# Expert weights: twenty of 104 low parts on GpSimd, 26 high parts on VectorE, and the first layer's last block as three 224-column products

## Chip, cores and metric

The kernel runs on one core of one Trainium2 chip. The metric is the device time of one execution in microseconds (us); a kernel's time is the median of its runs.

## What is computed

Three stages follow each other, in float32: attention with normalised queries and keys, a mixture of eight experts in which each expert takes at most 224 of 1792 tokens, and an MLP with the activation h * cos(h). The change lies in the second stage.

```python
def _moe_ref(x, w_gate, w1, w2):
    N, D = x.shape                      # 1792, 768
    E = w_gate.shape[1]                 # 8 experts, w1 768x1024, w2 1024x768
    cap = N // E                        # 224
    order = np.argsort(-(x @ w_gate).flatten())
    ...                                 # tokens go to experts in this order, 224 each
    for e in range(E):
        mask = assigned == e
        h = np.maximum(x[mask] @ w1[e], 0.0)
        out[mask] = h @ w2[e]
    return out
```

After it comes `h = x @ w_in; (h * cos(h)) @ w_out` for all 1792 tokens.

## The kernel before

**Two plans.** The kernel writes no engine's order by hand. Every operation becomes a `Step` with the engines that could run it (`ways`), its cost, and what it reads and writes. `Plan.run` then simulates all engines by these costs, picks at each moment a step by its due time, and emits the instructions in that order; on the chip each engine runs its own queue in that order and waits where data is missing. There is one plan for attention and one, called `second`, for the rest. A step with two ways goes to the engine that would finish it first. For that comparison the VectorE way is charged an extra `prefer` times its cost; `prefer` is the first number of `TUNE_B`, 1.75 before. `P.either` makes a step with a VectorE and a GpSimd way, but only while `P.shared` is true, and `moe` sets it to False (just above `fetch(0)`), so no low part has two ways before.

**Precision.** TensorE multiplies in fp32r, which keeps the high part of a float32. So each operand x is split into a high part (a copy in fp32r) and a low part (x minus the high part), and a product is hi*hi + hi*lo + lo*hi.

**An expert.** For experts 1 to 7, `expert(t, j)` first does eight blocks f of w1 (128 columns each, six pieces d of 128 rows) and then six blocks d of w2 (eight pieces f). I write expert 3's blocks as f0 to f7 and d0 to d5, and one piece as d0:6. Expert 0's first layer has no split. For every split block:

- `whole` issues a load from HBM into a ring of four stage tiles `ws` (SyncE queue, in order),
- `weights` (L1217) makes the high part, `wx<-ws`, on ScalarE or VectorE (two ways, also before), and the low part, `wx<-ws,wx`, on VectorE; `wx` is a ring of four tiles,
- TensorE does `two` per piece: the high part against 448 columns (the tokens' high and low parts side by side), then the low part against 224 columns,
- `halves` adds the two 224-column halves of the accumulator: a ScalarE copy of one half to `sm`, a VectorE addition,
- ScalarE writes the high part of the result and VectorE the low part: `gh<-sm` and `gh<-sm,gh` for w1 (with the relu), `x2h` and `x2l` for w2.

The pieces of w2's first block need all eight results of w1; the plan lets TensorE run pieces of d1 before d0:6 and d0:7, since f6 and f7 are the last to come.

**Beside it.** The router for the expert after next (`Router.slow`) runs at the same time on VectorE: it sends candidates to DRAM (`rows<-vm`), reads them back into all partitions with eight broadcast loads (`AB<-rows`, SyncE queue), and then takes eight steps of comparing (`oh<-AB`), counting and a small product. GpSimd issues the gathers of an expert's tokens (`xr<-x,idx`) and the scatters of results (`out_dram<-xo,idx`) and has nothing else to do in this part. Two experts are followed by an MLP over their 448 tokens, four times.

Of the kernel before, what the change touches and what calls it, by code (L numbers as in the profile page):

```python
# [12 lines left out]
F32 = mybir.dt.float32  # L13
# [4 lines left out]
ALU = mybir.AluOpType  # L18
# [32 lines left out]
class Plan:  # L51
# [99 lines left out]
    def ring(self, pool):  # L151

        def make(name, n, shape, dt=F32):
            tiles = [pool.tile(shape, dt, name=f"{name}{i}") for i in range(n)]
            at = [0]

            def take():
                at[0] += 1
                return tiles[(at[0] - 1) % n]
            return take  # L160
        return make
# [540 lines left out]
CP, NCOL, E, CAP = 112, 16, 8, 224  # L702
# [402 lines left out]
CP, E, CAP, DM, F1, F2 = 112, 8, 224, 768, 1024, 2048  # L1105
KD, K1, K2 = DM // 128, F1 // 128, F2 // 128
PT = 2 * CAP
C1 = 6.28125
C2 = 2.0 * math.pi - C1
TUNE_B = (1.75, 0.8, 2.6, 0.6, 7.0, 9e9)  # L1110
RUSH = (15.0, 4.0, 5.0)
QUICK = (0, 1)
WARM_B = 24
# [2 lines left out]
TURN = 5  # L1116
EARLIER = 140
MAGS = 4
GROUPS = [[0, 1], [2, 3], [4, 5], [6, 7]]


def moe(tc, P, R, ident, x_rows, w1, w2, w_in, w_out, out, narrow):

    nc = tc.nc
    with ExitStack() as ctx:
        cst = ctx.enter_context(tc.tile_pool(name="m_cst", bufs=1))
        pp = ctx.enter_context(tc.tile_pool(name="m_ps", bufs=1, space=PSUM))
        v, sc = P.vector, P.scalar
# [12 lines left out]
        xe = cst.tile([128, KD, PT], F32R, name="xe")  # L1141
        xf = cst.tile([128, KD, CAP], F32, name="xf")
        xo = cst.tile([CP, 4, DM], F32, name="xo")
        mags = ring("na", MAGS, [128, 4, 128], I32)
        x2h = cst.tile([128, KD, PT], F32R, name="x2h")
# [56 lines left out]
        def whole(src, c0, n, keys):  # L1202

            s = stage()[:, 0:n]

            def load():
                w = src()
                nc.sync.dma_start(s, w[:, c0:c0 + 128].rearrange("(k p) n -> p k n", p=128))

            P.add([("SP", 0.46, load)], keys, [s], dma=n * 0.182)  # L1210
            return s

        def weights(src, c0, n, keys):

            s, x = whole(src, c0, n, keys), parts()[:, 0:n]
            hi, lo = x[:, :, 0], x[:, :, 1]
            P.add([("ACT", 0.093 + n * 0.1067, lambda: nc.scalar.activation(hi, s, AF.Copy)),  # L1217
                   ("DVE", 0.07 + n * 0.0667, lambda: nc.vector.tensor_copy(hi, s))], [s], [hi])
            v.tensor_tensor(lo, s, hi.bitcast(F32), op=ALU.subtract)
            return hi, lo  # L1220

        def ready(src, k0, n, keys):
# [6 lines left out]
        def fresh(d, k0):  # L1229
            x = parts()  # L1230
            for k in range(k0, k0 + K1, 4):
                i = narrow.at["wo", d, k]
                if i >= EARLY:
                    raw = stage().rearrange("p k n -> p (k n)").bitcast(I32).rearrange("p (k n) -> p k n", k=4)
                    narrow.piece(P, i, raw, mags(), x[:, k - k0:k - k0 + 4])
            return x[:, :, 0], x[:, :, 1]

        def block(f):
            P.begin()
            f()  # L1240
            P.finish()
            chain.append(P.steps[-1])

        def three(p, hi, lo, xh, xl, first, last):
            P.tensor.matmul(p, hi, xh, start=first, stop=False)
            P.tensor.matmul(p, hi, xl, start=False, stop=False)
            P.tensor.matmul(p, lo, xh, start=False, stop=last)

        def two(p, hi, lo, x, first, last):
            P.tensor.matmul(p, hi, x, start=first, stop=False)  # L1250
            P.tensor.matmul(p[:, 0:CAP], lo, x[:, 0:CAP], start=False, stop=last)

        def halves(p):
            y = sums()
            sc.activation(y, p[:, CAP:PT], AF.Copy)
            v.tensor_tensor(y, p[:, 0:CAP], y, op=ALU.add)
            return y

        def expert(t, j):
            def of(w):  # L1260
                return lambda: w[bass.ds(ev[t], 1)].rearrange("o k n -> (o k) n")

            for f in range(K1):
                if t == 0:
                    s = whole(of(w1), f * 128, KD, [f"ev{t}"])
                    p = acc()[:, 0:CAP]
                    for d in range(KD):
                        block(lambda: P.tensor.matmul(p, s[:, d], xf[:, d], start=d == 0,
                                                      stop=d == KD - 1))
                else:  # L1270
                    hi, lo = weights(of(w1), f * 128, KD, [f"ev{t}"])
                    p = acc()[:, 0:PT]
                    for d in range(KD):
                        block(lambda: two(p, hi[:, d], lo[:, d], xe[:, d], d == 0, d == KD - 1))
                    p = halves(p)
                a, b = hT[:, f, 0:CAP], hT[:, f, CAP:PT]
                sc.activation(a, p, AF.Relu)
                v.scalar_tensor_tensor(b, p, 0.0, a.bitcast(F32), op0=ALU.max, op1=ALU.subtract)
            o = j * CAP
            for d in range(KD):  # L1280
                hi, lo = weights(of(w2), d * 128, K1, [f"ev{t}"])
                p = acc()[:, 0:PT]
                for f in range(K1):
                    block(lambda: two(p, hi[:, f], lo[:, f], hT[:, f], f == 0, f == K1 - 1))
                p = halves(p)
                a, b = x2h[:, d, o:o + CAP], x2l[:, d, o:o + CAP]
                sc.activation(a, p, AF.Copy)
                v.tensor_tensor(b, p, a.bitcast(F32), op=ALU.subtract)

        def mlp(grp, ahead):  # L1290
# [15 lines left out]
            for d in range(KD):  # L1306
                if grp is GROUPS[0] and narrow.at["wo", d, 0] >= EARLY:
                    both = [fresh(d, k0) for k0 in range(0, K2, K1)]
# [4 lines left out]
                if d == TURN:  # L1313
                    ahead()
                cut = w // 2 if last and grp is GROUPS[-1] else w
                for a in range(0, w, cut):
# [30 lines left out]
        def fetch(t, step=None):  # L1347
            if t < E:
                P.rush = RUSH[min(t, 2)]
                route(t, step)  # L1350
                P.rush = 0.0

        fetch(0)
        for grp in GROUPS:
            for j, t in enumerate(grp):
                if j:
                    fetch(t)
                expert(t, j)
            behind = chain[-EARLIER]
            mlp(grp, lambda: fetch(grp[-1] + 1, behind))  # L1360
        P.run(zip(chain, chain[1:]), *TUNE_B)

# [64 lines left out]
```

## Time and profile before

| | us |
|---|---|
| median of 3 runs | 1168.14 |
| lowest, highest | 1165.21, 1170.52 |
| the profiled execution | 1162.75 |
| its span, first to last instruction | 1160.8 |

The profile names groups of instructions as `out<-in` without buffer numbers. "Idle before" an instruction, in brackets, is how long its engine stood still and what ended that. PE is TensorE's matmuls, DVE is VectorE, ACT ScalarE, POOL GpSimd, SP SyncE's queue of DMA issues. A matmul's own duration includes its pipeline; how fast they follow each other is read from their starts.

### The profile page before, as it was taken

The numbers are of one execution on the slowest core, as the hardware profiler recorded it, in microseconds if no ns is written. First come the engines' busy times: TensorE is split into PE (matmuls) and PEld (weight loads), VectorE is DVE, ScalarE is ACT, GpSimd is POOL, SyncE is SP. The second block draws the span as 40 slices with busy tenths as digits, with TensorE's granted clock in tenths as the row PEclk, the third lists the DMA queues.
The fourth block names the chain that finished last, engine by engine and source line by source line (L and its number), as shares of the span: only waits on it lengthen the run. The fifth ranks groups of instructions, "written<-read, shape, count | busy, mean of one in ns | idle before, by whom it ended". The sixth has DMA issues, their size and how long they took to land.

```text
span 1160.8 us, 22190 instructions
## 1 busy us (share of the span) xinstructions
PE 1108.4 (95%) x7944; PEld 906.6 (78%) x7944; DVE 899.8 (78%) x2477; ACT 646.4 (56%) x1575; POOL 137.6 (12%) x288
## 2 busy tenths in 40 slices
PE   7999999999994989999999999999999999999996
PEld 5465665555552879899899899899899989999996
DVE  7888998999977978996997897578889578856401
ACT  4787787676663356663556574246666235746400
POOL 5361332331000000000001000001000000100001
PEclk9999999999996999999999999999999999999998
DMA  7236575655751589779669668838867956866761
GB/s 215 66 114 224 156 236 181 191 169 177 234 206 61 151 216 270 267 240 304 224 163 266 206 208 259 303 107 233 245 215 231 298 204 171 239 207 217 244 217 48
DMA packets 180815, 237.58 MB, mean 205 GB/s; under 512 B 14113, under 2 KB 156897, under 8 KB 175073
## 3 DMA queue, kind: packets, MB, share of 16 engines
q1 hardware_dynamic: 178144, 225.15, 62.6%
q0 software_dynamic: 2560, 11.01, 3.5%
q8 instruction: 62, 1.02, 0.4%
q14 instruction: 49, 0.39, 0.1%
HBM read 199.52 MB, written 36.52 MB: 203 GB/s over the span
## 4 chain that ended last, share of the span: by engine, by line
PE 45%; DVE 3%; DMA 2%; ACT 1%; issue 1%; POOL 0%; POOLq 0%; SPq 0%; ACTq 0%; DVEq 0%
PE acc L47 44%; DMA ws<-in_moe_w_dram 2%; PE tr L47 1%; DVE wx L47 1%; DVE na L47 1%; ACT wx L1217 1%; PE rt L47 1%; DVE oh L47 0%; DVE xo L47 0%; POOL out_dram L1337 0%; DVE xe L47 0%; POOLq L1423 0%; DVE gh L47 0%; DVE ind L47 0%; DVE sm L47 0%
## 5 line engine op out<-in xcount | busy, mean ns | idle before, releaser
L47 PE MATMUL acc<-gh,wx 128*128 128x448 f32 (+1 forms) x1568 | 360.4, 344 | 4.1 <-DVE gh L47 3.6
L47 PEld LDWEIGHTS acc<-gh,wx 128*128 128x128 f32 x1568 | 264.8, 190 | 22.1 <-DVE gh L47 5.8
L47 PE MATMUL acc<-x2h,wx 128*128 128x448 f32 x768 | 222.3, 368 | 0.0
L47 PEld LDWEIGHTS acc<-x2h,wx 128*128 128x128 f32 x768 | 144.5, 188 | 11.2
L47 PE MATMUL acc<-gl,wx 128*128 128x448 f32 (+1 forms) x400 | 143.2, 358 | 0.0
L47 PE MATMUL acc<-x2l,wx 128*128 128x448 f32 x384 | 140.1, 365 | 0.0
L47 DVE TENSOR_TENSOR wx<-ws,wx 128x768 fp32r<-128x768 f32 (+1 forms) x104 | 112.3, 1080 | 26.5 <-ACT wx L1217 23.7
L1217 ACT ACTIVATE wx<-ws 128x768 fp32r<-128x768 f32 (+1 forms) x104 | 97.8, 940 | 28.8 <-DMA ws<-in_moe_w_dram 13.3
L47 ACT ACTIVATE pf<-st 112x448 f32<-112x448 f32 x192 | 93.7, 539 | 34.1 <-PE st L47 33.4
L47 DVE TENSOR_REDUCE cm<-s 128x1 f32<-128x448 f32 x168 | 100.2, 618 | 14.1 <-PE s L47 12.1
L47 PE MATMUL acc<-xe,wx 128*128 128x448 f32 (+1 forms) x672 | 107.3, 320 | 0.1
L47 ACT ACTIVATE r<-r 128x448 f32<-128x448 f32 x128 | 74.1, 579 | 57.8 <-DVE r L47 56.0
L47 PEld LDWEIGHTS acc<-xe,wx 128*128 128x128 f32 x672 | 100.6, 189 | 5.3 <-DVE wx L47 0.6
L47 PE MATMUL st<-qq,kk 64*112 64x448 f32 x576 | 89.1, 387 | 0.9 <-ACT pf L47 0.9
L47 ACT ACTIVATE oh<-oh 128x896 bf16<-128x896 bf16 x48 | 45.6, 950 | 73.8 <-DVE oh L47 73.7
L1168 POOL DMA_INDIRECT xr<-x,idx x16 | 15.5, 966 | 582.7 <-issue 198.8
L47 PE MATMUL po<-pf,vr 112*64 112x448 f32 x384 | 83.4, 552 | 0.3 <-ACT pf L47 0.3
L47 PEld LDWEIGHTS acc<-gl,wx 128*128 128x128 f32 x400 | 75.4, 189 | 4.7
L47 PEld LDWEIGHTS acc<-x2l,wx 128*128 128x128 f32 x384 | 72.2, 188 | 5.2
L47 PEld LDWEIGHTS st<-qq,kk 64*112 64x112 f32 x576 | 49.1, 171 | 18.1 <-ACT pf L47 5.6
L47 ACT ACTIVATE sq<-qk 112x64 f32<-112x64 f32 (+1 forms) x195 | 57.6, 303 | 8.2 <-DVE rt L47 4.1
L47 DVE COPY xo<-tr 112x512 f32<-112x512 f32 (+1 forms) x25 | 16.5, 664 | 58.0 <-PE tr L47 56.4
(251 smaller groups left out, 1831.9 us busy)
## 6 DMA issues: line engine op xcount, KB each, us to landing
wx<-w_in SPq DMA_DIRECT2D x64, 768.0 KB
wx<-w_out SPq DMA_DIRECT2D x44, 1024.0 KB
ws<-in_moe_w_dram SPq DMA_DIRECT2D x64, 384.0 KB
ws<-in_moe_w_dram SPq DMA_DIRECT2D x48, 512.0 KB
nr<-in_moe_w_in_dram SPq DMA_DIRECT2D x32, 384.0 KB
w_in<-nr SPq DMA_DIRECT2D x32, 384.0 KB
nr<-in_moe_w_out_dram SPq DMA_DIRECT2D x16, 512.0 KB
w_out<-nr SPq DMA_DIRECT2D x16, 512.0 KB
```

The source lines that it names most:

```text
L47: self.plan.add([(self.eng, self.plan.cost(self.eng, name, out, r, kw), lambda: f(*args, **kw))], r, w)
L1168: P.add([("POOL", 2.1 - 0.9 * h, lambda x=x, h=h: nc.gpsimd.indirect_dma_start(out=x, out_offset=None, in_=x_rows, in_offset=bass.Indirect ...
L1217: P.add([("ACT", 0.093 + n * 0.1067, lambda: nc.scalar.activation(hi, s, AF.Copy)), ("DVE", 0.07 + n * 0.0667, lambda: nc.vector.tensor_co ...
```

## The change

One tuning number and two places in `moe` change:

```diff
-TUNE_B = (1.75, 0.8, 2.6, 0.6, 7.0, 9e9)
+TUNE_B = (0.8, 0.8, 2.6, 0.6, 7.0, 9e9)
...
+SHORT = (K1 - 1,)
...
-            v.tensor_tensor(lo, s, hi.bitcast(F32), op=ALU.subtract)
+            P.shared = True
+            P.either("tensor_tensor", lo, s, hi.bitcast(F32), op=ALU.subtract)
+            P.shared = False
...
-                    for d in range(KD):
-                        block(lambda: two(p, hi[:, d], lo[:, d], xe[:, d], d == 0, d == KD - 1))
-                    p = halves(p)
+                    if f in SHORT:
+                        p = p[:, 0:CAP]
+                        for d in range(KD):
+                            block(lambda: three(p, hi[:, d], lo[:, d], xe[:, d, 0:CAP], xe[:, d, CAP:PT], d == 0, d == KD - 1))
+                    else:
+                        for d in range(KD):
+                            block(lambda: two(p, hi[:, d], lo[:, d], xe[:, d], d == 0, d == KD - 1))
+                        p = halves(p)
```

The low parts get a second way, GpSimd. `prefer` also weighs the high parts' VectorE way, so these move too. In the built program 20 of the 104 low parts stand on GpSimd (13 of w1, 7 of w2) and 26 of the 104 high parts on VectorE (18 of w1, 8 of w2), where before all high parts stood on ScalarE and all low parts on VectorE. Block f7 of experts 1 to 7 accumulates in 224 columns and has no `halves`. Attention's order is the same, instruction by instruction; in the rest the plan sets all engines anew.

VectorE at the end of expert 3's first layer, before. `wx2`, `wx3`, `wx0`, `wx1` with x8x128 are the low parts of d0, d1, d2, d3; the `sm` rows are the additions for f5, f6, f7; the `gh` rows are the low parts of f4, f5, f6, f7; `oh` is the router's first comparison:

```order
L47 TENSOR_TENSOR wx2_4610<-ws2_4606,wx2_4610 128x8x128
L47 TENSOR_TENSOR sm1_4619<-acc3_4599,sm1_4619 128x224
L47 SCALAR_TENSOR_TENSOR gh_4631<-sm0_4618,gh_4631 128x224
L47 TENSOR_TENSOR wx3_4611<-ws3_4607,wx3_4611 128x8x128
L47 SCALAR_TENSOR_TENSOR gh_4631<-sm1_4619,gh_4631 128x224
L47 TENSOR_TENSOR sm0_4618<-acc0_4596,sm0_4618 128x224
L47 TENSOR_TENSOR wx0_4608<-ws0_4604,wx0_4608 128x8x128
L47 TENSOR_TENSOR sm1_4619<-acc1_4597,sm1_4619 128x224
L47 TENSOR_TENSOR wx1_4609<-ws1_4605,wx1_4609 128x8x128
L47 SCALAR_TENSOR_TENSOR gh_4631<-sm0_4618,gh_4631 128x224
L47 SCALAR_TENSOR_TENSOR gh_4631<-sm1_4619,gh_4631 128x224
L47 TENSOR_SCALAR oh_4651<-AB_4650,b0_80 128x896
```

The same place with the change (the `gh` rows are f5, f6, f7; `CAST` is the high part of d3):

```order
L47 TENSOR_TENSOR wx2_4610<-ws2_4606,wx2_4610 128x8x128
L47 TENSOR_TENSOR sm1_4619<-acc3_4599,sm1_4619 128x224
L47 TENSOR_TENSOR sm0_4618<-acc0_4596,sm0_4618 128x224
L47 SCALAR_TENSOR_TENSOR gh_4631<-sm1_4619,gh_4631 128x224
L47 TENSOR_SCALAR oh_4651<-AB_4650,b0_80 128x896
L47 TENSOR_TENSOR wx0_4608<-ws0_4604,wx0_4608 128x8x128
L1219 CAST wx1_4609<-ws1_4605 128x8x128
L47 SCALAR_TENSOR_TENSOR gh_4631<-sm0_4618,gh_4631 128x224
L47 SCALAR_TENSOR_TENSOR gh_4631<-acc1_4597,gh_4631 128x224
```

The low parts of d1 and d3 and the addition for f7 are gone from VectorE; the router's comparison and a high part have come in ahead of f6 and f7, and f7's low part reads the accumulator.

GpSimd's queue with the change, from the low part of expert 3's f4 to the gathers for expert 4 (before, nothing stood between the scatters and these gathers). The low parts are f4, f7, d1 and d3:

```order
L47 TENSOR_TENSOR wx2_4610<-ws2_4606,wx2_4610 128x6x128
L47 TENSOR_TENSOR wx1_4609<-ws1_4605,wx1_4609 128x6x128
L47 TENSOR_TENSOR wx3_4611<-ws3_4607,wx3_4611 128x8x128
L47 TENSOR_TENSOR wx1_4609<-ws1_4605,wx1_4609 128x8x128
L1169 DMA xr0_4620<-x_66,idx4_4637 112x768
L1169 DMA xr1_4621<-x_66,idx4_4637 112x768
```

Four low parts have come in behind the scatters of the first MLP; expert 5 has the same four.

SyncE's queue for expert 1, before (register moves and the load of f4 left out). The w1 rows are the loads of f1, f3, f5, f6, f7:

```order
L1208 DMA ws3_4607<-in_moe_w1_dram 128x6x128
...
L1208 DMA ws1_4605<-in_moe_w1_dram 128x6x128
...
L1208 DMA ws3_4607<-in_moe_w1_dram 128x6x128
L997 DMA rows_71<-vm_4652 112x8x16
...
L1208 DMA ws0_4604<-in_moe_w1_dram 128x6x128
L1000 DMA AB_4650<-rows_71 16x1792 x8
...
L1208 DMA ws1_4605<-in_moe_w1_dram 128x6x128
```

The same queue with the change; the w1 rows are the loads of f0, f2, f1, f3, f4:

```order
L1209 DMA ws2_4606<-in_moe_w1_dram 128x6x128
L997 DMA rows_71<-vm_4652 112x8x16
...
L1209 DMA ws0_4604<-in_moe_w1_dram 128x6x128
...
L1209 DMA ws3_4607<-in_moe_w1_dram 128x6x128
L1000 DMA AB_4650<-rows_71 16x1792 x8
...
L1209 DMA ws1_4605<-in_moe_w1_dram 128x6x128
...
L1209 DMA ws2_4606<-in_moe_w1_dram 128x6x128
```

The router's broadcasts have moved from between f6 and f7 to between f1 and f3. For experts 3 and 5 they stand where they stood, between f5 and f6.

## Rows read from the trace of the kernel before

**Rows 1.** The page, busy time, share of the span and instructions of two engines.
```profile
PE 1108.4 (95%) x7944; PEld 906.6 (78%) x7944; DVE 899.8 (78%) x2477; ACT 646.4 (56%) x1575; POOL 137.6 (12%) x288
```
**Rows 2.** Windows, second layers of experts 3, 5, 7: length; busy PE, PEld, DVE, ACT, POOL; clock.
```profile
636.25:653.57 17.32, 15.57 (x98) 14.28 (x97) 15.47 (x35) 11.17 (x24) 0.00 (x0) 1.00 0.67 207
825.39:842.59 17.20, 15.57 (x98) 14.28 (x97) 15.69 (x35) 11.04 (x24) 0.00 (x0) 1.00 0.69 216
1014.51:1029.60 15.09, 15.09 (x98) 14.26 (x97) 8.98 (x17) 7.19 (x16) 0.00 (x0) 1.00 0.60 189
```
**Rows 3.** Timeline of PE, the waits in the second layers of experts 3 and 1.
```profile
638.38 2.14 PE L47 MATMUL acc<-gh,wx 128*128 128x448 f32 x12 [0.40 <-DVE gh L47]
641.87 1.41 PE L47 MATMUL acc<-gh,wx 128*128 128x448 f32 x7 [1.35 <-DVE gh L47]
...
451.85 0.47 PE L47 MATMUL acc<-gh,wx 128*128 128x448 f32 x1 [0.21 <-DVE gh L47]
```
**Rows 4.** Timeline of SP in expert 3's first layer: issues with start and length.
```profile
618.71 4.07 SPq L1000 DMA_DIRECT2D AB<-rows  x8
623.35 15.07 SPq L1208 DMA_DIRECT2D ws<-in_moe_w_dram  x8
```
**Rows 5.** Timeline of ACT and DVE around the end of expert 3's first layer.
```profile
630.70 0.85 ACT L1217 ACTIVATE wx<-ws 128x768 fp32r<-128x768 f32 x1 [1.71 <-DMA ws<-in_moe_w_dram]
...
636.80 1.23 DVE L47 TENSOR_TENSOR wx<-ws,wx 128x1024 fp32r<-128x1024 f32 x1 [0.19 <-ACT wx L1217]
...
641.43 0.69 DVE L47 SCALAR_TENSOR_TENSOR gh<-sm,gh 128x224 fp32r<-128x224 f32 x2
642.03 0.68 DVE L47 TENSOR_SCALAR oh<-AB,b 128x896 bf16<-128x896 f32 x1
```
**Rows 6.** Groups by form: DVE's low parts, the nearest copy, POOL's two-input operation, ACT's high part.
```profile
L47 DVE TENSOR_TENSOR wx<-ws,wx 128x1024 fp32r<-128x1024 f32 x48 | 58.8, 1224 | 13.1 <-ACT wx L1217 11.9 <-issue 0.4
L47 DVE TENSOR_TENSOR wx<-ws,wx 128x768 fp32r<-128x768 f32 x56 | 53.5, 956 | 13.4 <-ACT wx L1217 11.8 <-issue 1.0
L47 DVE TENSOR_SCALAR na<-na 128x512 f32<-128x512 f32 x24 | 10.0, 418 | 1.5 <-ACT na L47 1.5
L47 POOL TENSOR_TENSOR qn<-qk,rs 112x512 f32<-112x512 f32 x42 | 45.5, 1090 | 123.4 <-PE t L47 112.4 <-issue 9.0 <-POOL mx L47 0.8
L1217 ACT ACTIVATE wx<-ws 128x1024 fp32r<-128x1024 f32 x48 | 50.7, 1057 | 14.1 <-DMA ws<-in_moe_w_dram 9.6 <-issue 4.4
```
**Rows 7.** Timeline in attention, POOL and DVE at the same time, two places.
```profile
78.71 2.19 POOL L47 TENSOR_TENSOR rt<-rs 112x48 f32<-112x48 f32 x1 [6.34 <-DVE rs L47]
80.97 0.29 POOL L47 TENSOR_TENSOR rt<-rt,ss 112x48 f32<-112x48 f32 x1
...
78.81 1.96 DVE L47 SCALAR_TENSOR_TENSOR na<-nr,na 128x384 int32<-128x384 int32 x4
...
86.72 1.04 POOL L47 TENSOR_TENSOR qn<-qk,rs 112x512 f32<-112x512 f32 x1
...
86.77 1.61 DVE L47 TENSOR_SCALAR na<-na 128x384 f32<-128x384 f32 x2
```
**Rows 8.** Timeline of PE: expert 1's first layer, and 224-column products of the last MLP.
```profile
432.99 15.20 PE L47 MATMUL acc<-xe,wx 128*128 128x448 f32 x96
448.03 3.61 PE L47 MATMUL acc<-gh,wx 128*128 128x448 f32 x22
...
1138.35 0.27 PE L47 MATMUL acc<-gl,wx 128*128 128x224 f32 x1
...
1140.36 0.27 PE L47 MATMUL acc<-gl,wx 128*128 128x224 f32 x1
```
**Rows 9.** Timeline of PE in expert 0's second layer; a window behind it (clock third from last).
```profile
421.56 0.41 PE L47 MATMUL tr<-ident,xr 112*128 112x112 f32 x2 [2.56 <-DMA xr<-x,idx]
...
423.36 0.96 PE L47 MATMUL acc<-gh,wx 128*128 128x224 f32 x2 [0.55 <-DVE wx L47]
...
423.40:427.00 3.60, 3.60 (x16) 3.41 (x17) 3.57 (x10) 2.30 (x6) 0.00 (x0) 0.58 0.46 136
```
## Prediction

> **What bounds the kernel now.** I read the page first: TensorE is busy in 95% of the span, VectorE in 78%, GpSimd in 12% [rows 1]. The page says which engine is full, not where there is air, so next come the starts of matmuls, searched for pauses. Both MLP layers have almost none. The pauses from expert 0's second layer on lie where an expert goes from its first layer to its second; the windows show them. Expert 7's second layer, with no router beside it, takes 15.09 us and has no pause; experts 3 and 5 take 17.32 and 17.20 us with PE busy for 15.57 in both [rows 2]. The difference of 1.75 and 1.63 us is all that a perfect change could win there, beside router products that stay.
>
> The timeline of PE puts expert 3's pauses at two places, 0.40 and 1.35 us, both ended by VectorE's `gh`, the low part of a first-layer result [rows 3]. The reader should ask why VectorE was late. It starts with a load: ScalarE stood 1.71 us until the weights of f6 arrived at 630.70 [rows 5], and that load left SyncE only at 623.35, behind eight broadcasts of the router issued over 4.07 us [rows 4]. After it ScalarE and VectorE work off a backlog, and the low parts for f6 and f7 end last, from 641.43 on [rows 5]. Expert 5 does the same. Expert 1 loses 0.21 us in this way [rows 3]. Expert 0 waits 2.56 us for gathered tokens and 0.55 us for a low part, and then runs 3.6 us at a granted clock of 0.58, between the two levels of 1.2 and 2.4 GHz [rows 9].
>
> So PE can gain some 4 us in experts 1, 3 and 5 and a few more in expert 0, of 1168. The question is whether VectorE's relief reaches those pauses.
>
> **The change part by part.** *Three products instead of two in f7.* Expert 1's first layer is 48 pieces in 448.03 - 432.99 = 15.04 us, 0.313 us a piece [rows 8]. A piece of three 224-column products appears in the last MLP: six follow each other from 1138.35 to 1140.36, 0.335 us each (first and last row of six steps [rows 8]). Six pieces in each of seven experts: 42 x 0.022 = **+0.9 us**, all on PE. The gain, f7's ScalarE copy and VectorE addition, counts only if f7 ends last; behind f6 in VectorE's queue it does not.
>
> *Prices of the moved work.* A low part costs VectorE 0.956 us (768 elements) and 1.224 us (1024) [rows 6]. GpSimd shows none. Its nearest row is `qn`, two inputs, 512 elements, 1.04 us [rows 7]; in proportion 1.57 and 2.09 us. From below VectorE's own price bounds it; from above the 48-element operation at 0.29 us [rows 7] taken in proportion, 4.6 and 6.2 us. I take the proportion of `qn`, nearest in size, and keep the rest for the range. A high part on VectorE: nearest is `na`, one input, 512 elements, 0.418 us [rows 6], so 0.63 and 0.84 us; the bounds are 0.418 itself and ScalarE's 1.057 [rows 6]. VectorE thus sheds 13 x 0.956 + 7 x 1.224 = 21.0 us and takes on 18 x 0.63 + 8 x 0.84 = 18.1 us. Summed over all, VectorE is hardly relieved; ScalarE is, and it is no bound (11.17 us busy of 17.32 [rows 2]).
>
> *GpSimd and VectorE get in each other's way.* A POOL operation of 48 elements took 2.19 us at 78.71, while VectorE ran four two-input operations back to back from 78.81; the like one behind it took 0.29 us. The other way round, two one-input VectorE operations of 384 elements took 1.61 us together, while POOL did a `qn` of 1.04 us from 86.72 [rows 7]; of 512 elements one takes 0.418 us [rows 6]. So while a low part runs on GpSimd, VectorE's operations with two operands in SBUF, and its fast copies, wait for its end; those that read PSUM do not seem to. The Trainium skill, "GPSIMD Engine Reference", section "Key points", says the same: GpSimd's SBUF interfaces are shared with VectorE, with contention from two-SBUF-input and two-port instructions. By that rule a low part moved to GpSimd does not free VectorE, and the sum stays as I make it; without it the next paragraph's 2.5 us fall away. The same page's section that reconciles its model with measured numbers has 4497 ns for a two-input operation of 2048 elements; an estimate from it is 1.7 and 2.2 us, which would make the sum below some 0.5 us larger.
>
> *Experts 3 and 5.* The loads and broadcasts stand as they stood, so the backlog starts as before. The high part of d1 is ready at 636.80 [rows 5]; GpSimd takes its low part and is done at 638.9. Behind that waits VectorE's low part for f5, `gh<-sm,gh`, two operands in SBUF: done about 639.3, where PE now resumes at 638.38 [rows 3], +1.0 us. Then VectorE has, in the order shown, the comparison (0.68), d2's low part (1.22), d3's high part (0.84) and f6's low part (0.38), each following some 0.09 us early: about 642.05, so PE resumes at 642.15 instead of 641.87 [rows 3]. By then it has done d0:0 to d0:5 and two pieces of d1, not five as before: 0.28 + 3 x 0.313 = 1.2 us late. Two experts: **+2.5 us**. Without the contention, f5's low part is on time and the end comes out within 0.1 us of before.
>
> *Expert 1.* The broadcasts go ahead of f3, so f7's load is no longer behind them; the 0.21 us go: **-0.2 us**. *Expert 0.* Two pieces of d4 now stand before d3 in PE's queue and fill 0.6 us of the wait for d3. Against it, d0's low part on GpSimd stands ahead of the gather of expert 1's tokens, and d4's load waits for that low part's end: some 0.6 us. **0 us**, bounds -2 (the low clock goes too: 3.6 us at 0.58 cost 1.5) and +2 (another such stretch). *Experts 2, 4, 6, 7.* Expert 7 shows that the queues have air there (DVE 8.98 of 15.09 us [rows 2]); the copies that VectorE takes on are hidden: 0. If that cover were gone, four copies of 0.63, 2.5 us an expert. *The scatters* now have low parts in front or behind, but nothing waits for a scatter soon: 0.
>
> The sum: 0.9 + 2.5 - 0.2 + 0 = **+3.2 us**. Against the profiled execution that is 1162.75 + 3.2 = 1165.9; that execution lies 5.4 us below the median of the runs shown, so against the median: **1171.3 us**, 0.3% more. About 0.5%, 5.8 us, is what a measurement here can tell from no change.
>
> **The rivals.** *B, the relief works.* If GpSimd and VectorE overlap freely, and the plan's order then lets f5, f6 and f7 come early, the pauses of experts 1, 3 and 5 go: 0.9 - 0.2 - 1.75 - 1.63 = -2.7, so 1165.4; with expert 0's clock (1.5) and half of its waits (1.6), 1162. For it: half of VectorE's operations here read PSUM. Against it: [rows 7], and the router's comparison ahead of f6.
>
> *C, slower by a late load.* In expert 1 the eight broadcasts now hold up f3 and all behind it. In expert 3 the load behind them left at 623.35 and was used at 630.70, 7.35 us later [rows 4, 5]. PE needs f3 at 432.99 + 18 x 0.313 = 438.6; high and low part take 1.8 us, so it decides whether f3's load leaves after 429.5. f1's load waits for d3's low part, ready about 423.3 [rows 9]; with 4.07 us of broadcasts the load leaves about 428. Each us beyond 429.5 costs one, and f4 to f7 follow: if the broadcasts themselves wait 3 to 5 us for `rows`, PE stands 1.5 to 3.5 us, three times over in the worst order, and may fall to the low clock once more, 1.5 us by [rows 9]: with the forecast's 3.2 some 1178. *D, nothing.* The order shows that the change does what it says, so this is no rival by itself; contention that costs half of what I charge gives +2, inside the forecast.
>
> **How the numbers follow.** The forecast has 0.56 (1168 to 1175, by the bounds of GpSimd's price and expert 0), B 0.27 (1161 to 1168), C 0.17 (1174 to 1182). The range 1163 to 1177 leaves out the ends of B and C, two in ten. Faster by over 0.5% needs B with expert 0's clock and waits: 0.08. Slower by over 0.5% needs C or the forecast's upper end: 0.17. The same: 0.75.
>
> **What would show it.** Right: POOL `wx<-ws,wx` x20 near 1.6 and 2.1 us; beside them VectorE's `gh<-sm,gh` and `wx<-ws` copies of over 1 us; PE's pauses on `gh` in experts 3 and 5 as long or longer; first layers 0.13 us longer each. Wrong: these pauses gone and the VectorE rows of old length (B), or PE waiting for `wx` in expert 1's first layer behind `ws` loads (C). A new wait in experts 2, 4, 6 or 7, or in an MLP, would be a cause that I have not seen.

## The result

The changed kernel takes 1178.66 us in the median of 5 runs (1175.79 to 1180.29), the kernel before 1167.84 us: a ratio of 1.0094, 95% interval 1.0068 to 1.0119, or 10.8 us slower. The forecast was 1171.3 us and a range up to 1177.0; the time lies above both.

The page of the changed kernel's profiled execution (1179.76 us), busy time of the engines, to be read against [rows 1]:

```profile
span 1177.9 us, 22305 instructions
...
PE 1117.2 (95%) x7986; PEld 915.0 (78%) x7986; DVE 914.8 (78%) x2476; ACT 629.4 (53%) x1542; POOL 179.5 (15%) x308
```

GpSimd has 41.9 us more and VectorE, from which twenty low parts were taken, 15.0 us more, not less. The groups by form show why (x counts, then busy us and mean ns of one):

```profile
L47 POOL TENSOR_TENSOR wx<-ws,wx 128x768 fp32r<-128x768 f32 x13 | 24.2, 1860 | 264.4 <-ACT wx L1218 188.2 <-DMA ws<-in_moe_w_dram 58.9 <-DVE sm L47 12.1
L47 POOL TENSOR_TENSOR wx<-ws,wx 128x1024 fp32r<-128x1024 f32 x7 | 17.1, 2447 | 45.7 <-ACT wx L1218 33.7 <-PE acc L47 6.6 <-DVE wx L1219 5.4
L1219 DVE CAST wx<-ws 128x1024 fp32r<-128x1024 f32 x8 | 7.1, 899 | 0.0
L47 DVE SCALAR_TENSOR_TENSOR gh<-sm,gh 128x224 fp32r<-128x224 f32 x49 | 26.6, 542 | 1.9 <-ACT gh L47 1.9
L47 DVE TENSOR_TENSOR x2l<-sm,x2h 128x224 fp32r<-128x224 f32 x48 | 26.5, 552 | 7.1 <-ACT x2h L47 6.6 <-issue 0.5
```

In a second trace of the kernel before, two of these rows are

```profile
L47 DVE SCALAR_TENSOR_TENSOR gh<-sm,gh 128x224 fp32r<-128x224 f32 x56 | 21.3, 384 | 1.5 <-ACT gh L47 1.5
L47 DVE TENSOR_TENSOR x2l<-sm,x2h 128x224 fp32r<-128x224 f32 x48 | 18.2, 387 | 5.8 <-ACT x2h L47 5.7
```

so a `gh` or `x2l` row is on average 0.16 us longer, and single ones are far longer, as in expert 3's second layer. Its timeline in the changed kernel, GpSimd, then VectorE, then PE:

```profile
641.07 1.89 POOL L47 TENSOR_TENSOR wx<-ws,wx 128x768 fp32r<-128x768 f32 x1 [6.71 <-ACT wx L1218]
645.71 2.38 POOL L47 TENSOR_TENSOR wx<-ws,wx 128x1024 fp32r<-128x1024 f32 x1 [2.75 <-ACT wx L1218]
...
641.40 1.80 DVE L47 SCALAR_TENSOR_TENSOR gh<-sm,gh 128x224 fp32r<-128x224 f32 x1 [0.16 <-ACT gh L47]
...
646.22 2.12 DVE L47 SCALAR_TENSOR_TENSOR gh<-sm,gh 128x224 fp32r<-128x224 f32 x1
648.25 0.67 DVE L47 TENSOR_SCALAR oh<-AB,b 128x896 bf16<-128x896 f32 x1
...
648.38 1.20 PE L47 MATMUL acc<-gh,wx 128*128 128x448 f32 x6 [1.56 <-DVE gh L47]
651.02 2.50 PE L47 MATMUL acc<-gh,wx 128*128 128x448 f32 x7 [1.44 <-DVE gh L47]
```

The `gh` row that starts at 646.22 ends at 648.34, just after GpSimd's row (645.71 + 2.38 = 648.09), and PE resumes at 648.38. PE stands 3.0 us here, against 1.75 us in [rows 3]. In expert 1, where PE stood 0.21 us [rows 3], GpSimd's low part of d2 (450.90, 2.39 us) stops VectorE's copy for d3, and the results of f6 and f7 come behind it:

```profile
451.48 2.37 DVE L1219 CAST wx<-ws 128x1024 fp32r<-128x1024 f32 x1
...
454.50 6.76 PE L47 MATMUL acc<-gh,wx 128*128 128x448 f32 x31 [2.31 <-DVE gh L47]
```

The windows add what no row of a wait shows. Second layers of experts 1, 3 and 5, and a piece of expert 3's (length; busy PE, PEld, DVE, ACT, POOL; clock third from last):

```profile
450.07:470.52 20.45, 17.49 (x102) 15.90 (x100) 18.88 (x40) 8.15 (x20) 5.15 (x2) 0.92 0.72 234
644.89:666.76 21.87, 18.87 (x100) 16.90 (x99) 18.80 (x38) 11.13 (x23) 4.77 (x2) 0.84 0.54 169
651.02:656.60 5.58, 5.58 (x20) 5.00 (x20) 4.80 (x7) 2.14 (x5) 2.17 (x1) 0.50 0.05 14
839.33:859.14 19.81, 17.39 (x101) 15.84 (x99) 18.35 (x36) 10.34 (x22) 4.79 (x2) 0.91 0.59 186
```

Behind the two pauses of expert 3 PE worked at the lower level (1.2 GHz, 0.50 in the third row). (1 - 0.92) x 20.45 + (1 - 0.84) x 21.87 + (1 - 0.91) x 19.81 is 6.9 us; in both traces of before the clock stays at 1.00 in these layers, for experts 3 and 5 in [rows 2].

From the starts of each stage's first product, the changed kernel's trace against the two of before: expert 1's second layer is 4.6 and 4.0 us longer (20.45 against 15.87 and 16.48), expert 2's 1.7 and 0.9, expert 3's 4.4 and 3.8, expert 5's 2.5 and 2.2; expert 0's two layers together 0.1 and 0.3, experts 4, 6 and 7 within 0.4. The rest is attention and the MLPs. Attention, up to expert 0's first product, takes 390.0 us here and 388.3 in both traces of before, but 388.0 to 390.9 in the eleven runs below that keep the order of before; the MLPs take 505.4 us together, against 504.4 and 509.3. So no loss can be read off there.

### The profile page after: what moved, and what is told of

Same layout as the page of the kernel before. It is cut to its first block, busy times and chain, and to the rows that moved or that the text cites. A ratio compares the mean times of both kernels' runs of the same rounds, so it can differ in the third digit from the quotient of the medians.

```text
span 1177.9 us, 22305 instructions
## 1 busy us (share of the span) xinstructions
PE 1117.2 (95%) x7986; PEld 915.0 (78%) x7986; DVE 914.8 (78%) x2476; ACT 629.4 (53%) x1542; POOL 179.5 (15%) x308
## 3 DMA queue, kind: packets, MB, share of 16 engines
q8 instruction: 63, 1.03, 0.4%
## 4 chain that ended last, share of the span: by engine, by line
PE 73%; DVE 15%; DMA 6%; ACT 2%; issue 2%; POOL 1%; SPq 0%; POOLq 0%; DVEq 0%; ACTq 0%
PE acc L47 50%; PE st L47 6%; PE po L47 5%; DMA ws<-in_moe_w_dram 4%; PE dn L47 3%; PE s L47 3%; PE t L47 3%; DVE oh L47 2%; DVE wx L47 2%; DVE cm L47 2%; DVE na L47 1%; PE tr L47 1%; PE rt L47 1%; DVE AB L47 1%; PE dn L418 1%
## 5 line engine op out<-in xcount | busy, mean ns | idle before, releaser
L47 PE MATMUL acc<-gh,wx 128*128 128x448 f32 (+1 forms) x1568 | 367.4, 349 | 9.5 <-DVE gh L47 9.4
L47 PEld LDWEIGHTS acc<-gh,wx 128*128 128x128 f32 x1568 | 269.9, 193 | 28.7 <-DVE gh L47 11.4
L47 DVE TENSOR_REDUCE cm<-s 128x1 f32<-128x448 f32 x168 | 100.3, 619 | 14.1 <-PE s L47 12.1
L47 DVE TENSOR_TENSOR wx<-ws,wx 128x1024 fp32r<-128x1024 f32 (+1 forms) x84 | 91.0, 1085 | 24.4 <-ACT wx L1218 22.1
L47 POOL TENSOR_TENSOR wx<-ws,wx 128x768 fp32r<-128x768 f32 (+1 forms) x20 | 41.3, 2066 | 310.1 <-ACT wx L1218 221.8
L1218 ACT ACTIVATE wx<-ws 128x768 fp32r<-128x768 f32 (+1 forms) x78 | 74.2, 953 | 23.6 <-DMA ws<-in_moe_w_dram 13.6
L47 POOL TENSOR_TENSOR qn<-qk,rs 112x512 f32<-112x512 f32 x42 | 45.5, 1090 | 124.4 <-PE t L47 113.4
L47 ACT ACTIVATE o<-acc 128x448 f32<-128x448 f32 (+1 forms) x25 | 13.2, 529 | 93.7 <-PE tr L47 70.6
```

Of the source, the lines that this page charges most:

```text
L47: self.plan.add([(self.eng, self.plan.cost(self.eng, name, out, r, kw), lambda: f(*args, **kw))], r, w)
```

## Experiments

**First batch: is it GpSimd, or the order?** All four ran on one chip; before had 1167.19 us (17 runs).

*All low parts back on VectorE, in the changed order.*

```diff
-        for _, _, f in sorted(out, key=lambda o: o[:2]):
+        for _, i, f in sorted(out, key=lambda o: o[:2]):
+            s = self.steps[i]
+            if s.name in BACK and s.eng == "POOL":
+                f = s.ways[0][2]
             f()
```

> The changed kernel with every queue in the changed order, but the twenty low parts that the change put on GpSimd are issued on VectorE, each at the place in VectorE's queue where its planned start puts it. Nothing else differs. Theory 1 (blocking: while GpSimd makes a low part, VectorE's next operation with two operands in SBUF, or its copy from SBUF, waits for the end, and that is what makes PE late in experts 0, 1, 3 and 5): most of the loss goes, some 6 to 10 us of the 10.8, so 1169 to 1173 us, 0.1 to 0.4% over before; the pauses of 1.7 to 1.8 us in expert 3 and of 2.6 us in expert 1 shrink by 0.5 to 1 us each, the low-clock stretches behind them go, and the 1.96 us in expert 2, where no low part is on GpSimd, stays. Theory 2 (the new order itself is at fault, whichever engine makes the low parts): within 2 us of the changed kernel, 1177 to 1181 us.

Measured: 1178.42 us, ratio 1.0099 (1.0081 to 1.0117), the changed kernel's time. So theory 1 as I wrote it fell: in this order, moving twenty low parts from VectorE to GpSimd brings no gain and no loss that these runs can tell; the two intervals leave nearly 4 us open. Its profiled execution was its fastest run (1172.79 us) and shows pauses in the same experts. PE in expert 3's second layer, then the windows of the second layers of experts 3 and 5:

```profile
642.29 1.20 PE L48 MATMUL acc<-gh,wx 128*128 128x448 f32 x6 [0.20 <-DVE gh L48]
644.93 0.57 PE L48 MATMUL acc<-gh,wx 128*128 128x448 f32 x2 [1.44 <-DVE gh L48]
646.37 0.88 PE L48 MATMUL acc<-gh,wx 128*128 128x448 f32 x4 [0.86 <-DVE gh L48]
...
640.36:658.91 18.55, 16.04 (x100) 14.38 (x99) 17.05 (x38) 10.29 (x23) 0.00 (x0) 1.00 0.61 186
831.90:852.20 20.30, 17.65 (x100) 15.73 (x99) 17.21 (x39) 10.45 (x23) 0.00 (x0) 0.92 0.59 184
```

The pause of 1.44 us is as long as with GpSimd at work, so the order makes it: the comparison, d2's low part and d3's high part stand between the results of f5 and f6. The first one is 0.20 in place of 1.56 us, and a third of 0.86 us comes in, behind d3's low part, which now stands on VectorE ahead of f7's result. Expert 3 stands 2.5 us in all with the clock at 1.00; expert 5, with pauses of 0.36, 1.43 and 0.86 us, has 0.92. So the lengths of the pauses do not tell by themselves whether the clock falls, and what it costs differs between like stages.

*The same, with GpSimd making 17 of them once more* (the edit against the changed kernel; `s.name[1]` is the second making).

```diff
-        for _, _, f in sorted(out, key=lambda o: o[:2]):
-            f()
+        for _, i, f in sorted(out, key=lambda o: o[:2]):
+            s = self.steps[i]
+            if s.name and s.eng == "POOL":
+                s.ways[0][2]()
+                if s.name[0] not in ("e2f0", "e4f2", "e6f2"):
+                    s.name[1]()
+            else:
+                f()
```

> As the run with all low parts back on VectorE, and GpSimd makes 17 of the 20 a second time, at the place and with the operands that they have in the changed kernel, into memory that nobody reads in this part. So VectorE is relieved of nothing and GpSimd works as in the change. Theory 1 (blocking): 5 to 10 us slower than the run without the second making, 1176 to 1182 us, with VectorE rows of 1.8 to 2.4 us beside the GpSimd rows as in the changed kernel. Theory 2 (order): as the run without it, within 1 us.

Measured: 1200.97 us, 1.0285 (1.0262 to 1.0309), 22.5 us over the run without them, 1.3 us for each. Theory 2 as I wrote it fell too: GpSimd's work does cost. Both together: a low part costs about the same on either engine, which VectorE standing while GpSimd works would explain. The second making also reads stage and weight tiles and so may hold their buffers longer; the third batch has a run without that.

*The three products alone*, planned anew:

```diff
+SHORT = (K1 - 1,)
...
+                    if f in SHORT:
```

> The kernel before with block f7 of experts 1 to 7 as three 224-column products and nothing else of the change. By the prediction's term: 42 pieces of 0.022 us more, +0.9 us, 0.08%, and the pauses in experts 3 and 5 as before. If f7's missing copy and addition matter, these pauses shrink by up to 0.8 us each and the sum is -0.7 us. Either is within 0.2% of before. A loss of over 0.4% would say that the three products reorder the plan for the worse.

Measured: 1171.30 us, 1.0036 (1.0025 to 1.0047), over the price. *The tuning number alone*, planned anew:

```diff
-TUNE_B = (1.75, 0.8, 2.6, 0.6, 7.0, 9e9)
+TUNE_B = (0.8, 0.8, 2.6, 0.6, 7.0, 9e9)
```

> The kernel before with the first tuning number at 0.8 and nothing else: twenty high parts move to VectorE, no low part leaves it, and the plan sets all engines anew. By the prediction: the copies are covered, 0 us, within 0.2% of before. Theory 2 (order: earlier router steps and copies ahead of the low parts of results): a pause of some 2 us in expert 2 and longer ones in experts 1, 3 and 5, +3 to +8 us, 0.3 to 0.7% over before.

Measured: 1172.16 us, 1.0037 (1.0024 to 1.0050), theory 2's number, but at other places: experts 4 and 6 are 4.2 us longer in their second layers (a pause of 2.60 us in the one, of 1.60 and 0.64 us in the other, and a clock of 0.92 in each).

**Second batch: the moves in the order of before.** Here the plan runs with before's steps and costs, and only what a step issues is exchanged, so that every other instruction of every queue stands as before. Before had 1167.52 us (21 runs).

```diff
+            if name in HIGH:
+                swap(P.steps[-1], lambda: nc.vector.tensor_copy(hi, s))
             v.tensor_tensor(lo, s, hi.bitcast(F32), op=ALU.subtract)
+            if name in LOW:
+                swap(P.steps[-1], lambda: nc.gpsimd.tensor_tensor(lo, s, hi.bitcast(F32), op=ALU.subtract))
...
+        def swap(step, f):
+            step.ways = [(e, c, f) for e, c, _ in step.ways]
```

> The whole change in the order of before: the same twenty low parts on GpSimd, the same 26 high parts on VectorE and f7 as three products, each issued at the place where the plan of before has that step; every other instruction of every queue stands as before. Theory A (the new order costs, the moves by themselves little): less than half of the change's loss, 0 to +4 us over before. Theory B (blocking by GpSimd and the third product cost, whatever the order): +8 us or more, as the changed kernel or worse.

> The kernel before with the same twenty low parts on GpSimd at the places where VectorE had them in the plan, nothing else moved. If relief of VectorE were worth what it saves (13 x 0.956 + 7 x 1.224 = 21.0 us of VectorE time), the pauses in experts 3 and 5 would go: -2 to -4 us. If VectorE stands while GpSimd works (rows of 1.8 to 2.4 us beside GpSimd's), nothing is gained: 0 to +5 us.

> The kernel before with f7 of experts 1 to 7 as three products in the order of before. By price alone: +0.9 us (42 x 0.022), with 0.13 us more in each first layer, and at most -0.5 us in experts 3 and 5, where f7's low part no longer waits for a copy and an addition. The kernel with this part alone and a plan of its own was 4.2 us slower than before: theory A says that the difference between the two, some 3 us, is the order; if this run is 4 us slower too, it is the product.

> The kernel before with the 26 high parts of the change on VectorE, at the places where the plan of before has them on ScalarE. By price alone: copies of 0.55 and 0.69 us in VectorE's queue that are covered in experts 2, 4, 6 and 7 and stand ahead of low parts of results in experts 1, 3 and 5: 0 to +2 us. The kernel with the tuning number alone and a plan of its own was 5.0 us slower than before in the medians; theory A: most of that is the order.

| in the order of before | us | ratio (95%) |
|---|---|---|
| three products | 1168.21 | 0.9999 (0.9985 to 1.0013) |
| 26 high parts on VectorE | 1172.27 | 1.0041 (1.0028 to 1.0055) |
| 20 low parts on GpSimd | 1183.16 | 1.0130 (1.0104 to 1.0156) |
| all three | 1186.92 | 1.0153 (1.0128 to 1.0177) |

The three products cost nothing that can be told. In the trace a first layer without a pause is 0.13 us longer, as priced, and the second layers of experts 3 and 5 are 1.3 and 0.6 us shorter than in the second trace of before (0.7 and 0.3 us than in the first), which fits f7's result needing one copy and one addition less. The low parts cost 15.6 us, 0.78 us each. Not all of that need be VectorE standing: in this run's trace 3.5 to 4.2 us are lost in expert 2's second layer, where the clock is 0.92 and PE waits for gathered tokens, 0.26 us in the second trace of before:

```profile
618.36 0.51 PE L47 MATMUL tr<-ident,xr 112*128 112x112 f32 x3 [2.62 <-DMA xr<-x,idx]
```

GpSimd's two gathers there took 1.74 and 1.58 us, 0.94 each in the first trace of before; in the changed kernel they took 1.76 and 1.63 us. No low part is made beside them, and why they were slow is open. So theory A fell: the moves themselves cost, and the plan of the changed kernel, which knows GpSimd's price but not that VectorE stands meanwhile, even spares a part of it.

**Third batch: what of GpSimd stops VectorE, and the broadcasts.** Before had 1168.23 us (23 runs). Two kernels are that of before with 17 extra operations of GpSimd on memory that nobody needs then:

```diff
+        def beside(hi, n):
+            spare = gl[:, 13:16].rearrange("p f n -> p (f n)")
+            nc.gpsimd.tensor_copy(tag, hi[:, 0, 0:1].bitcast(F32))
+            nc.gpsimd.tensor_tensor(spare[:, 0:n * 128], spare[:, 0:n * 128].bitcast(F32), spare[:, 0:n * 128].bitcast(F32), op=ALU.subtract)
```

> The kernel before, every queue as it was and all low parts on VectorE. GpSimd gets 17 extra pairs: a one-element copy that waits for the high part of a block (those blocks of experts 0, 1, 3, 5 and 7 whose low parts the change puts on GpSimd), and behind it a two-input subtraction of 768 or 1024 elements on memory that nobody needs in this part. It holds back no buffer of the weights. If GpSimd's two-input operation stops VectorE's operations on SBUF: 17 stretches of about 1.8 or 2.4 us, +8 to +20 us over before, with gh and x2l rows of about 2 us. If GpSimd's work is free beside VectorE: 0 to +1 us.

> As the run with the extra subtractions, but GpSimd fills 2240 or 2688 elements with zeros in their place, for about as long, and reads nothing but the one element. If what stops VectorE is the reading of two operands: 0 to +1 us over before. If any work of GpSimd on SBUF stops it: the same loss as with the subtraction.

Measured: 1184.08 us with the subtraction, 1.0127 (1.0111 to 1.0143), 0.9 us each; 1170.27 us with the fill, 1.0019 (1.0005 to 1.0032). The fills take about as long (2.34 us where the longer subtraction takes 2.68, 1.97 where the shorter takes 1.60). GpSimd's rows by form, the subtractions:

```profile
L1238 POOL TENSOR_TENSOR gl<-gl 128x1024 fp32r<-128x1024 f32 x7 | 18.8, 2679 | 0.0
```

and the fills:

```profile
L1236 POOL MEMSET gl<- 128x2688 f32 x7 | 16.4, 2342 | 0.0
```

So it is not GpSimd's being busy but its reading that stops VectorE's two-input operations. Timelines of GpSimd and VectorE in expert 3, with the subtraction:

```profile
646.21 2.88 POOL L1238 TENSOR_TENSOR gl<-gl 128x1024 fp32r<-128x1024 f32 x1
...
647.27 2.08 DVE L47 SCALAR_TENSOR_TENSOR gh<-sm,gh 128x224 fp32r<-128x224 f32 x1
```

and with the fill:

```profile
645.63 2.34 POOL L1236 MEMSET gl<- 128x2688 f32 x1
...
645.57 0.69 DVE L47 SCALAR_TENSOR_TENSOR gh<-sm,gh 128x224 fp32r<-128x224 f32 x2
646.17 2.28 DVE L47 TENSOR_SCALAR oh<-AB,b 128x896 bf16<-128x896 f32 x1
```

Beside the fill two `gh` rows take 0.69 us as ever; only the one-input comparison `oh`, 0.68 us elsewhere [rows 5], takes 2.28 us.

*The broadcasts behind the loads of f6 and f7* (experts 3 and 5, a move in SyncE's queue alone):

```diff
+            if name and name[0] == "AB" and name[1] in (4, 6):
+                out[n] = ([o[0] for o in loads if o[0] > st][2-1] + 1e-6 + st * 1e-9, i, f)
```

> The kernel before with one thing moved: in experts 3 and 5 the eight broadcasts of the router stand in SyncE's queue behind the loads of f6 and f7 in place of ahead of them. If the prediction's reading of the pauses there is right, f6's load leaves some 2 us earlier, the 1.35 us pause and most of the 0.40 us go in both experts, and the broadcasts, 4 us later, are still in time for the first comparison at 642.03: -2 to -3.4 us, 0.2 to 0.3% faster than before. If another wait stands behind it (the first comparison, or the loads of d0 and d1): 0.

Measured: 1173.55 us, 1.0035 (1.0020 to 1.0050), slower. f6 is on time, and ScalarE waits for d0 instead:

```profile
638.72 1.06 ACT L1227 ACTIVATE wx<-ws 128x1024 fp32r<-128x1024 f32 x1 [4.25 <-DMA ws<-in_moe_w_dram]
```

*The change without its GpSimd way*, planned anew, against the changed kernel:

```diff
-            P.shared = True
-            P.either("tensor_tensor", lo, s, hi.bitcast(F32), op=ALU.subtract)
-            P.shared = False
+            v.tensor_tensor(lo, s, hi.bitcast(F32), op=ALU.subtract)
```

> The changed kernel without a GpSimd way for the low parts, planned anew: the tuning number at 0.8 and f7 as three products, 22 high parts on VectorE, all low parts on VectorE. The number alone cost 5.0 us and the three products nothing in the old order: 0 to +5 us over before, 0.2 to 0.5%. The rest up to the change's loss is what the GpSimd way adds, some 6 us. If instead it is as slow as the changed kernel, GpSimd's part in that plan costs nothing beside the order.

Measured: 1174.09 us, 1.0040 (1.0025 to 1.0055). In plans of their own, number and products cost 0.40% and the GpSimd way another 0.54%, some 0.3% either way.

**Fourth batch.** Before had 1169.31 us (22 runs). *One broadcast load in place of eight*, in the old order and planned anew:

```diff
+            src = rows.unsqueeze(1).to_broadcast([E, 16, NCOL * CP])
+            sync.dma_start(V, bass.AP(rows.tensor, rows.offset, [[NCOL * CP, E], [0, 16], [1, NCOL * CP]]))
```

> The kernel before with the router's eight broadcast loads as one load that writes all 128 partitions, at the place of the first; every other instruction as before. If the loads behind the broadcasts are what makes f6 late in experts 3 and 5 (the prediction's reading; moving the broadcasts behind f6 and f7 only handed the wait to d0), SyncE is free some 3.5 us earlier and the pauses there go: -2 to -3.5 us, 0.2 to 0.3% faster. If the wait is for the stage tiles or the transfer itself: within 0.1% of before.

> The same one load, told to the plan as one step of SyncE, so that all queues are planned anew. The mechanism gives the same -2 to -3.5 us; what a new order costs by itself was between -2 and +4 us so far (the three products alone: 0 in the old order, 4.2 us in a new one). So -5 to +2 us.

Measured: 1190.89 us, 1.0183 (1.0155 to 1.0210), and 1194.63 us, 1.0198 (1.0171 to 1.0225). The one issue takes 0.66 us, but f6's load, issued at 625.97, is used at 638.08, 12.1 us later, against 7.35 us before [rows 4, 5]. The window behind the issue has the DMA share (second from last) low:

```profile
626.00:628.00 2.00, 2.00 (x15) 1.92 (x14) 1.52 (x4) 0.89 (x3) 1.78 (x4) 1.00 0.63 184
```

In before it is 0.95 to 1.03 in the windows from 619 to 625, around its eight broadcasts. So the wait here is for transfers, not for SyncE's issue time, and this form of the load is slower than eight. The Trainium skill, "DMA: Bandwidth & Descriptors", section "Why a DMA increments its semaphore by 16 and not by 1", says that the slowest dimension of both sides sets how many of the 16 engines a DMA uses. On the side of `rows` it has 8 entries here; the fall to 0.63 fits that, but no run here counts the engines. In this trace the second layers of experts 1, 3 and 5 take 15.15, 15.42 and 15.65 us, near expert 7's 15.09, while their first layers grew to 20.41, 19.45 and 19.63 us with clocks of 0.91 and 0.92: the wait moved and grew. The run is thus no clean test of SyncE's issue time.

*22 of the 26 high parts* and *5 of the 20 low parts*, each alone and in the old order, by the lists that the second batch's edit reads (the first list goes without the four of expert 2):

```diff
+HIGH = ("e1d3", "e1d4", "e1d5", "e3f4", "e3f5", "e3d3", "e4f4", "e4f5", "e4f6", "e5f4", "e5f5", "e5d3", "e6f4", "e6f5", "e6f6", "e6d4", "e7f4", "e7f5", "e7f6", "e7f7", "e7d4", "e7d5")
```
```diff
+LOW = ("e2f0", "e4f2", "e6f2", "e7f1", "e7f4")
```

> The kernel before with 22 of the 26 high parts on VectorE, in the old order: expert 2's four stay on ScalarE. All 26 cost 4.75 us. If what they cost is VectorE's time where PE waits for it, expert 2 (where the router's one-hot rows for expert 3 are late by these copies, a pause of 1.39 us and a first layer of 2.9 us more) has 2 to 3 us of it: +2 to +3 us over before. If each copy costs alike: 22 of 26, +4 us.

> The kernel before with five low parts on GpSimd in the old order: those of the change in experts 2, 4, 6 (made during an MLP) and 7. All twenty cost 15.6 us, 0.78 us each. If a low part on GpSimd costs only where PE waits for what VectorE does next, these five cost nothing: within 0.1% of before, though VectorE's rows beside them are as long as elsewhere. If each costs alike: +3.9 us, 0.33%.

Measured: 1167.98 us, 0.9991 (0.9973 to 1.0008), and 1172.58 us, 1.0027 (1.0008 to 1.0045). The high parts cost where they delay something PE waits for: without expert 2's four nothing is left of the 4.75 us. There, with all 26, PE waited 1.13 us for a row of the router (`pv`, from VectorE, with copies ahead of it), and the first layer's clock was 0.91 in the mean (1.00 before):

```profile
601.84 0.94 PE L47 MATMUL rt<-pv,oh 112*112 112x6 bf16 x16 [1.13 <-DVE pv L47]
```

The five low parts cost 3.3 us, 0.65 us each, although I took their places for free: in MLP time too PE waits for what VectorE does next (a router step of 0.17 us took 1.81 us beside GpSimd's row at 776.82, and the transposes behind it came 1.62 us late).

*A version meant to beat both:* before, with f7 as three products in experts 3 and 5 alone, and there d3's parts behind the results of f6 and f7. Before had 1167.40 us (17 runs).

```diff
+            for part, behind in (("hi", "gh"), ("lo", "gl")):
+                n = at[f"e{t}d3", part]
+                out[n] = (max(out[n][0], out[at[f"e{t}f7", behind]][0] + 1e-6),) + out[n][1:]
```

> A version meant to beat both. The kernel before with f7 as three products in experts 3 and 5 alone, and there ScalarE's and VectorE's parts of d3 behind the first-layer results of f6 and f7 (in before they stand ahead of them, and ScalarE's waits for d3's load meanwhile). PE stood 1.35 us there; with the results no longer behind a part of 1.06 and one of 1.23 us the pause should shrink to 0.1 to 0.5 us: -0.9 to -1.3 us in each of the two experts, +0.3 us for the two blocks of three products: -1.5 to -2.3 us, 0.13 to 0.2% faster, at the edge of what can be told. If d3 then comes late for PE: 0.

Measured: 1164.97 us, 0.9978 (0.9968 to 0.9988), 2.4 us faster than before and the fastest of all. Windows of the second layers of experts 3 and 5 in the second trace of before:

```profile
637.29:655.33 18.04, 15.73 (x101) 14.32 (x99) 15.57 (x35) 11.72 (x24) 0.00 (x0) 1.00 0.66 206
828.08:845.68 17.60, 15.72 (x100) 14.31 (x99) 15.56 (x35) 10.95 (x24) 0.00 (x0) 1.00 0.67 216
```

and in this kernel:

```profile
640.48:656.28 15.80, 15.57 (x101) 14.40 (x99) 14.61 (x33) 10.59 (x23) 0.00 (x0) 1.00 0.73 228
828.34:843.80 15.46, 15.39 (x101) 14.40 (x99) 14.41 (x33) 10.28 (x22) 0.00 (x0) 1.00 0.73 235
```

Both layers come near the 15.09 us of expert 7 [rows 2]. They are 2.2 and 2.1 us shorter than in the second trace of before, and 1.7 and 1.9 than in the first; with the three products in the old order alone they took 16.75 and 17.03 us. The further 0.9 and 1.6 us go with the place of d3's parts in the two queues, four instructions in all; no run moved these parts alone.

*The kernel before once more*, unchanged, for a second trace.

> The kernel before once more, for a second trace. Its first profiled execution took 1162.75 us, some 5 us under the median of its runs. If that execution was an early one, this one takes 1165 to 1170 us, and the difference stands in attention and expert 0 and in the router's waits of the MLPs, as in the traces of the variants whose order is that of before; the second layers of experts 3 and 5 take 17.3 to 17.5 us again.

Measured: 1169.85 us. Against the first trace (1162.75) experts 3 and 5 differ by 0.6 and 0.3 us in their second layers; the third MLP's second layer is 4.0 us longer, 2.37 us of it in one wait for the router. So MLP stages of single traces can't be compared to better than that, stages of experts 1 to 7 to some 0.8 us, and expert 0's two layers only as a sum (they differ by +2.5 and -2.7 us). PE in expert 3's second layer:

```profile
640.21 2.14 PE L47 MATMUL acc<-gh,wx 128*128 128x448 f32 x12 [1.18 <-DVE gh L47]
643.47 1.72 PE L47 MATMUL acc<-gh,wx 128*128 128x448 f32 x9 [1.12 <-DVE gh L47]
```

It stood 2.3 us here, and the clock of the layer stayed at 1.00 (the window from 637.29 above).

## Why the prediction was wrong

**Three products, +0.9 us.** Price right: 0.13 us in each first layer without a pause. Experts 3 and 5 had shorter second layers, which the term left out; the runs give 0 with 1.5 us open either way, so they cannot tell 0.9 from 0.

**GpSimd's price.** Taken 1.57 and 2.09 us, measured 1.86 and 2.45 us, inside the bounds. The estimate of 2.2 us beside it would by the prediction's own working move each of the two experts by 0.15 us, 0.3 us and not 0.5.

**Contention.** Right in kind. VectorE's rows of over 1 us stand beside GpSimd's as listed. By the rule of the Trainium skill's "GPSIMD Engine Reference" the low part moved would not free VectorE, and the run with all of them back on VectorE agrees: no difference that the two intervals can tell.

**Experts 3 and 5, +2.5 us.** The pauses came out as worked: expert 3 stands 3.0 in place of 1.75 us, +1.25 where I had +1.2. That agreement is in part luck: with these low parts on VectorE the same place stands 2.5 us, so by that trace GpSimd adds 0.5 us to what the order does, while the prediction had the end within 0.1 us of before without the contention. What failed is the step from pauses to time: "1.2 us late" counted only the standing. Pauses of 1.56 and 1.44 us were followed by 5.58 us at a clock of 0.50. In the two traces of before, pauses of 0.40 and 1.35 us [rows 3] and of 1.18 and 1.12 us were not followed by a lower clock, nor were 0.20, 1.44 and 0.86 us with the low parts back. Which pauses the clock falls behind is open. Against the first trace of before the two layers lost 4.4 and 2.5 us, 3.5 and 1.8 of them by the clock.

**Expert 1, -0.2 us.** This step failed most: +4.0 to +4.6 us. It looked at SyncE's loads alone and left out what stands in VectorE's queue ahead of the results of f6 and f7, with d2's low part on GpSimd and a VectorE copy held behind it: 2.31 us of pause, and 1.6 us of clock. GpSimd is not the whole of it: with that low part on VectorE the layer still took 19.50 us (pauses of 1.49 and 0.62 us, clock 0.91).

**Experts 2, 4, 6, 7, 0 us.** Expert 2 lost 0.9 to 1.7 us: its d2 load landed late for ScalarE, PE stood 1.69 us. That four copies could cost 2.5 us an expert was the text's own bound for cover gone; the run with 26 high parts showed it in expert 2. The tuning number alone cost 4.2 us in experts 4 and 6, but there the order is new too; with the copies in the old order their second layers took 16.80 and 16.83 us, as before. **Expert 0, 0 us:** +0.1 to +0.3 in sum, though its first layer lost 0.8 to 3.3 us (PE waited 3.26 us for a router product whose one-hot rows stood beside d0's low part on GpSimd) and its second gave it back.

**Rival C** has the measured time, 1178, but not its mechanism: f3's load did leave late, at 431.92, and f3's high part was made at 438.15, still ahead of PE's first f3 piece at 440.53; expert 1's first layer took 15.2 us. The layer began 1.9 us later than before, at 434.89, and the load was used after 6.2 us, not 7.35. **Rival B** fell with the two runs on GpSimd. **The reading of the pauses** in experts 3 and 5 was half right: the late load starts the backlog, but moving the broadcasts away from f6's load only handed the wait to d0, while with d3's parts behind the results the pauses went.

How much of the 10.8 us belongs to which part has no single answer: the parts add up to 1.0170 in the old order (measured together 1.0153), to 0.40 and 0.54% in plans of their own, and the changed order costs the same, as far as these runs can tell, with the low parts on VectorE. That the new order by itself costs is shown by the three products (0.9999 and 1.0036), at which places it would in another plan is open.

## What to carry to other kernels

Before work is moved from VectorE to GpSimd, look at what VectorE runs beside it: if these are operations with two operands in SBUF, the move may free nothing, as here. Price a pause of TensorE together with the clock that may fall behind it: in the second layers of experts 1, 3 and 5 it cost 6.9 us, where the standing grew by 3.7 to 4.8 us. When a list scheduler sets the order, test each part of a change in the old order too, and look at the two or three instructions ahead of the one that is late: with f7 of two experts as three products, that gained here 2.4 us, what twenty moved operations did not.

## What the runs showed of the hardware

GpSimd's fill, which reads nothing, left two-input operations of VectorE at their length (0.69 us for two) and stopped only a one-input one (2.28 in place of 0.68 us); its two-input subtractions stopped both kinds (a `gh` of 2.08 us in the run with the extra ones, a one-input copy of 2.37 us beside d2's low part in the changed kernel). The prediction had made no difference by what GpSimd reads. The Trainium skill, "SBUF — State Buffer", section "Who interferes with whom", has this distinction, and the two runs agree with it. It goes both ways: beside two two-input operations of VectorE that kept their 0.69 us, GpSimd's low part of 768 elements took 3.06 us (at 572.37 in the run with five low parts), not 1.86.
